# Clustered attention and two MLPs on one core: head 0's scores unsplit, GpSimd's wide passes in halves, one written-out order

## The chip, the cores and the metric

The kernel runs on one core of a Trainium2 chip. The metric is device microseconds of one execution. Before the change the median of three runs is 760.87 us (759.79 to 761.59). The profile is of one further execution, which took 763.72 us itself, with a span of 761.8 us from the first to the last instruction.

## The reference

Three parts run one after the other on float32 data.

```python
# attention: 2 batches x 8 heads = 16 heads, 768 positions, 64 wide
mask = q_assign[:, :, :, None] == k_assign[:, :, None, :]   # argmax over 16 centroids
scores = np.where(mask, scale * np.matmul(q, k.transpose(0, 1, 3, 2)), -1e9)
attn = softmax(scores)                # max, exp, sum
x = (attn @ v) reshaped to [1536, 512]
# first MLP
h = ((x @ w1) * (x @ w2)) @ w3 @ w_out        # 512 -> 1024 -> 1024 -> 512
# second MLP
h = x @ w_in ; g = h * clip(h + 3, 0, 6) / 6 ; out = g @ w_out   # 512 -> 2048 -> 512
```

## The kernel before, in words

A float32 product is built from float32r matmuls. Each operand is split into a high part and a rest, and three products (high by high, high by rest, rest by high) are summed in PSUM. The split costs an ACT copy (the high part) and a DVE or POOL subtraction (the rest) for every tile.

**Attention.** The 16 heads follow one another. For head h, `load_qk` (L1167) loads q and k, `qk_T` transposes them on PE, `qk_hi` and `qk_lo` split them, DMAs (`move_kh`, `move_kl`, `move_qh`) put the parts of k and q where a single matmul sums two of the three products, `assign_mm` (L1228) multiplies by the centroids, and nine steps `oh0` to `oh8` on DVE and POOL make a one-hot code of the cluster, which is appended to q and k (`Ck`, `Cq`), so that the mask comes out of the score matmul. `scores` (L1323) makes one chunk of 128 queries by 768 keys in two parts, `S1` (512 keys) and `S` (256). Chunks alternate between the halves of one PSUM tile of three banks, so that neighbours share the middle bank: `S` of a chunk waits for the exp of the chunk before. `smax` (L1340) takes the row maximum on DVE, `sexp` (L1348) the exp on ACT, with the row sum. `p_T` transposes the exp, `p_hi` and `p_lo` (L1379) split it, `av` (L1382) multiplies by v.

Head 0 is an exception in the kernel before (`WHOLE = 1`): its exp and v are left whole in float32, so that its `av` is a plain float32 matmul, which the profile shows as two instructions each, and it has no `p_lo`. Its scores are split as all others are.

Two heads make a pair. For a pair, POOL adds the two halves of the sums (`o_sum`, L1412, the operation `os`), multiplies by the reciprocal of the row sums (`pair_mul`, L1443, `pm`), and DVE or POOL splits the result (`pair_hi`, `pair_lo`, L1457, `xh` and `xl`). Each of these is one pass over 128x768.

**The MLPs.** Beside the attention, weights arrive from HBM, and five steps on ACT, POOL and DVE convert each tile of 128x512: `c0` (ACT), `c1` (`c_clamp`, L1567, a POOL pass), `c2` (ACT), `c3` and `c5` (DVE, two SBUF inputs each). w3 is multiplied by w_out ahead (`w`, L1629), then x by w1 and w2 (`ab`, L1705, batch 0; `b`, L1957, batch 1), then by that product (`x2`, L1820). The second MLP takes 16 steps: `h` (L2268) seven products for a block of w_in, with snapshots and sums on ACT and DVE between them, `hr`, `hm`, `hh`, `hl` the activation and its split, `o` (L2312) the product with w_out. The splits of its operands are `xs` (`x_sum`, L2229), `xwl` (`x_lo`, L2235), `Ll` (`l_lo`, L2182) and `wol2` (`w_lo`, L2192), on DVE or POOL.

**The order.** Every operation is an entry of `Plan` with an engine (or a choice of engines), a duration, what it needs, a due time and the buffers that it takes and gives back. `Plan.order` (L888) is a planner: it steps through time with these durations and latencies, and of the operations that can start takes the one due first. A table `SHIFT` with one number for nearly every operation moves the due times. Each engine then executes its operations in the order in which the planner emitted them; nothing overtakes.

`warm` (L1089) is a one-column activation that exists to bring a table into ACT: `root` does it with Sqrt, `warm` with Exp. `idle_pe` (L1117) issues matmuls without use, 21 in all.

Of the kernel before, what the change touches and what calls it, by code (L numbers as in the profile page):

```python
# [44 lines left out]
SHIFT = {  # L45
    "id": 8.27, "root": -37.83, "warm": -0.72, "cenl": -28.31, "cen1": -21.13, "cen2": -11.74, "cen3": 0.22,
    ("idle", 0): 0.14, ("idle", 1): 14.27, ("idle", 7): -19.93, ("idle", 8): 1.32, ("cT", 0): -2.63,
    ("cTc", 0): -18.72, ("cTc", 1): 38.21, ("lq", 0): -20.58, ("lk", 0): -6.84, ("vhi", 0): 13.43,
    ("vlo", 0): -8.33, ("T", 0, 0): -2.21, ("qkh", 0, 0): -20.39, ("qkl", 0, 0): -48.81, ("T", 0, 1): 58.8,
# [820 lines left out]
class Plan:  # L870
# [10 lines left out]
    def op(self, key, eng, dur, fn, need=(), due=0.0, take=(), drop=(), lat=0.0, lock=False, after=()):  # L881
        assert key not in self.ops, key
        if isinstance(eng, str):
            eng, dur = (eng,), (dur,)
# [1535 lines left out]
```

## Time and profile before

| | us |
|---|---|
| median of the runs | 760.87 |
| profiled execution | 763.72 |
| its span | 761.8 |
| PE busy | 739.7 |
| DVE busy | 617.8 |
| ACT busy | 551.5 |
| POOL busy | 209.9 |

A line of the timeline gives the start and the length in us, the engine, the line of the kernel, the operation, the tile written and the tiles read, the form, and in brackets how long the engine had been idle and what released it. POOL is GpSimd, DVE is VectorE, ACT is ScalarE, PE is TensorE. SPq is the queue that issues the DMAs. A matmul's length is its latency; matmuls that follow one another overlap.

### The profile page before, as it was taken

Reading aid. Unit: us, or ns where it says so; the run is one execution under the profiler, and the core shown is the slowest. Engines: PE = TensorE matmul, PEld = TensorE weight load, DVE = VectorE, ACT = ScalarE, POOL = GpSimd, SP = SyncE. Lnnn points to the kernel's source line nnn. Section 1 sums busy time; section 2 is a strip of 40 time slices with the busy share of each in tenths; the row PEclk is TensorE's granted clock in tenths of the full one; section 3 lists DMA queues with packets and bytes.
Section 4 is the critical chain, followed back from the end, with each engine's and each line's share of the span. In section 5 each row is a group of like instructions: output and inputs, shape, how many; then the busy total and the mean of one; then the engine's idle time right before and its main releaser. Section 6 shows DMA issues by size and latency. Waiting matters only on the chain.

```text
span 761.8 us, 12047 instructions
## 1 busy us (share of the span) xinstructions
PE 739.7 (97%) x4143; PEld 673.7 (88%) x4143; DVE 617.8 (81%) x1032; ACT 551.5 (72%) x1037; POOL 209.9 (28%) x232
## 2 busy tenths in 40 slices
PE   5899998999999999999999999999999999999998
PEld 4679887889899998999999999988988888988896
DVE  7778898999988887878896998979878867676642
ACT  6788898888889777878756767668765756565553
POOL 2441645252445435351341301322203000000000
PEclk9999999999999999999999999999999999999999
DMA  8745554565546646342536534685431224222102
GB/s 223 225 128 163 146 146 118 156 160 136 151 124 173 170 127 182 113 137 84 159 100 193 178 125 139 196 264 192 157 103 37 76 70 135 83 60 78 47 1 97
DMA packets 81740, 101.96 MB, mean 134 GB/s; under 512 B 30960, under 2 KB 56592, under 8 KB 81680
## 3 DMA queue, kind: packets, MB, share of 16 engines
q1 hardware_dynamic: 81680, 101.20, 45.0%
q8 instruction: 33, 0.54, 0.3%
q14 instruction: 27, 0.22, 0.1%
HBM read 71.34 MB, written 15.78 MB: 114 GB/s over the span
## 4 chain that ended last, share of the span: by engine, by line
PE 82%; DVE 6%; ACT 5%; DMA 4%; issue 2%; SPq 0%; POOL 0%; DVEq 0%; ACTq 0%; POOLq 0%
PE po L2312 15%; PE psh L2268 13%; PE av L1390 8%; PE psx L1820 8%; PE pst L1332 8%; PE ptr L1367 7%; PE psab L1705 7%; PE psab L1957 7%; PE psw L1629 5%; DMA qkn<-in_k_dram 1%; PE pa L1233 1%; PE ptqk L1194 1%; DVE den L1344 1%; PE pt L1601 1%; DMA rdb<-rd 1%
## 5 line engine op out<-in xcount | busy, mean ns | idle before, releaser
L1569 POOL TENSOR_SCALAR cvt<-cvt 128x512 f32<-128x512 f32 x72 | 67.3, 938 | 192.0 <-ACT cvt L1013 178.1
L1344 DVE TENSOR_REDUCE den<-pst 128x1 f32<-128x768 f32 x96 | 91.5, 953 | 22.8 <-PE pst L1332 18.1
L1351 ACT ACTIVATE p<-pst,den 128x768 f32<-128x768 f32 x96 | 86.6, 902 | 17.8 <-DVE den L1344 16.9
L1010 DVE TENSOR_TENSOR pl<-ptr,ph 128x512 fp32r<-128x512 f32 x135 | 89.4, 680 | 9.4 <-ACT ph L1013 9.1
L1013 ACT ACTIVATE ph<-ptr 128x512 fp32r<-128x512 f32 x135 | 78.7, 596 | 18.6 <-PE ptr L1367 13.8
L1367 PE MATMUL ptr<-id_f,p 128*128 128x128 f32 x576 | 81.3, 272 | 0.9 <-DVE pl L1010 0.6
L1705 PE MATMUL psab<-xT,abhl 128*128 128x384 f32 x384 | 78.9, 342 | 0.3 <-ACT asb L1013 0.3
L1367 PEld LDWEIGHTS ptr<-id_f,p 128*128 128x128 f32 x576 | 68.2, 140 | 8.8 <-DVE pl L1010 0.9
L1332 PE MATMUL pst<-kk,qkL 128*128 128x512 f32 (+1 forms) x192 | 71.0, 378 | 3.1 <-ACT p L1351 3.0
L1705 PEld LDWEIGHTS psab<-xT,abhl 128*128 128x128 f32 x384 | 66.2, 188 | 2.3 <-ACT asb L1013 0.8
L1332 PE MATMUL pst<-kk,qkH 128*128 128x512 f32 (+1 forms) x192 | 64.9, 342 | 0.0
L1390 PE MATMUL av<-pl,vs 128*128 128x384 f32 x180 | 61.3, 341 | 2.3 <-DVE pl L1010 2.3
L1390 PE MATMUL av<-ph,vs 128*128 128x384 f32 x180 | 63.3, 351 | 0.2 <-ACT T L1013 0.2
L1578 DVE SCALAR_TENSOR_TENSOR cvs<-cvt,cvs 128x512 int32<-128x512 int32 x72 | 52.4, 735 | 12.7 <-ACT cvs L1013 6.4
L1013 ACT ACTIVATE cvt<-raw 128x512 f32<-128x512 f32 x72 | 48.2, 672 | 11.5 <-DVE cvs L1582 3.8
L2290 ACT ACTIVATE tt<-m_sn,three 128x384 f32<-128x384 f32 x48 | 29.4, 615 | 37.0 <-DVE m_sn L2278 27.7
L1013 ACT ACTIVATE cvs<-raw 128x512 int32<-128x512 uint8 x72 | 47.9, 673 | 6.7 <-DMA set<-cvs 5.2
L1582 DVE SCALAR_TENSOR_TENSOR cvs<-cvt,cvs 128x512 int32<-128x512 int32 x72 | 51.2, 719 | 0.4
L1629 PE MATMUL psw<-woh,wT 128*128 128x512 f32 x128 | 49.3, 411 | 0.0
L1332 PEld LDWEIGHTS pst<-kk,qkL 128*128 128x128 f32 x192 | 36.9, 192 | 9.8 <-ACT p L1351 8.0
L1013 ACT ACTIVATE m_sn<-psh 128x384 f32<-128x384 f32 x64 | 30.8, 483 | 20.0 <-PE psh L2268 19.9
L2312 PE MATMUL po<-m_whl,m_gv 128*128 128x512 f32 x153 | 40.6, 392 | 0.6 <-DVE m_gv L1010 0.6
(198 smaller groups left out, 1829.6 us busy)
## 6 DMA issues: line engine op xcount, KB each, us to landing
raw<-in_moe_w_dram SPq DMA_DIRECT2D x32, 512.0 KB, 3.6
m_gb<-set SPq DMA_DIRECT2D x64, 256.0 KB, 3.3
raw<-in_moe_w_out_dram SPq DMA_DIRECT2D x24, 512.0 KB, 3.5
raw<-in_moe_w_in_dram SPq DMA_DIRECT2D x16, 512.0 KB, 5.1
set<-cvs SPq DMA_DIRECT2D x32, 256.0 KB, 3.1
kk<-qkH SPq DMA_DIRECT2D x16, 384.0 KB, 4.2
abp<-cvs SPq DMA_DIRECT2D x16, 256.0 KB, 2.3
b_gv<-abp SPq DMA_DIRECT2D x16, 256.0 KB, 4.4
```

The source lines that it names most:

```text
L1010: nc.vector.tensor_tensor(out=out, in0=a, in1=b, op=ALU.subtract)
L1013: nc.scalar.activation(out=out, in_=in_, func=AF.Copy, **kw)
L1332: x = mm(out=psr[:, t, ks_], lhsT=TT[nm, h][:, i, cs_], rhs=flat(TT["K", h][:, a])[:, ks_], start=st, stop=sp)
L1344: done["mx", n] = [other_banks(nc.vector.tensor_reduce(out=den_at(h, 0, c), in_=psS[h, c], axis=AX.X, op=ALU.max, negate=True), ("S", n + 1))]
L1351: done["ex", n] = [other_banks(nc.scalar.activation(out=flat(p), in_=psS.pop((h, c)), func=AF.Exp, bias=den_at(h, 0, c), accum_out=den_at( ...
L1367: nc.tensor.transpose(pt[:, blk(j)], pps[h, 3 * hf + c][:, blk(kb)], id_f)
L1390: mm(out=t[:, 0:HF], lhsT=vs_t[h][:, 2 * s + i, :], rhs=x_[:, c0:c0 + HF], start=(s == 0 and i == 0 and n == 0), stop=(s == 2 and i == 1 a ...
L1569: (nc.gpsimd.tensor_scalar if e == "pool" else ts)(out=tf, in0=tf, scalar1=H_MAX, scalar2=-H_MAX, op0=ALU.min, op1=ALU.max)
L1629: mm(out=ps, lhsT=wT[m, hf][:, a, blk(kk)], rhs=w_[hf][:, kk, :], start=(kk == 0 and n == 0), stop=(kk == 3 and n == 2))
L1705: mm(out=ps[:, 0:HF], lhsT=s[:, w, a, blk(kk)], rhs=xT0[0][:, x_, kk, hf * HF:hf * HF + HF], start=(kk == 0 and n == 0), stop=(kk == KD - ...
L2268: mm(out=ps[:, 0:HF], lhsT=left(p, l, a, kk), rhs=x[:, x_, kk, :], start=(st and kk == 0 and m == 0), stop=(kk == 1 and m == 2), skip_grou ...
L2312: mm(out=outs[b, c], lhsT=g[:, a, blk(c % 3)], rhs=w[:, w_, :], start=(first and a == 0 and w_ == 0), stop=(last and a == 1))
```

## The change

The planner, its latencies and `SHIFT` go. `RANK` gives every operation its place in one list of 3968, and `ON` the engine where there is a choice. The families are listed in the order in which their operations are created (by head, by chunk, and so on). `order` sorts by rank and asserts that needs and buffers hold.

```diff
-SHIFT = {
-    "id": 8.27, "root": -37.83, "warm": -0.72, "cenl": -28.31, "cen1": -21.13, "cen2": -11.74, "cen3": 0.22,
...
+RANK = {
+    "id": "7",
+    "root": "246",
+    "warm": "217",
...
+    "idle": "12 58 109 137 39 47",
...
+    "lq": "2 4 36 76 151 457 321 616 709 946 927 1188 1180 1430 1613 1668",
+    "lk": "11 19 62 146 361 486 519 714 773 965 970 1216 1388 1466 1650 1719",
+    "lv": "1 14 169 399 602 673 475 808 919 1224 1117 1462 1386 1580 1742 1900",
...
+    "os": "349 415 619 688 854 917 1111 1169 1397 1419 1610 1693 1954 1965",
+    "pm": "429 439 695 707 931 936 1178 1182 1439 1447 1674 1740 1975 1983 2157 2164",
...
+    "xwl": "2707 2758 2750 2746 2767 2779 2776 3100 3245 3185 3270 3225 3239 3369",
+    "xs": "2716 2726 2754 2761 3132 3218 3219 3280",
...
+ON = {
+    "Ck": "da",
+    "Cq": "aa",
+    "oh1": "ppppppppppdppdd",
+    "oh4": "ppdppppppppppdp",
+    "xh": "ppap",
+    "c1": "ppdpddppdppppdppppppppppppppdpppppppppdpdddpddddpppppppppdddpddpddddpddp",
...
+    "Ll": "ddddddddddddddddddpddpdddddddppd",
+    "wol2": "ddddpdddddddddpppppddddpddddpddp",
+    "xwl": "pddddddddddpdp",
+    "xs": "ddddpppp",
```

Of `c1`, 25 of 72 passes go from POOL to DVE. Of the passes of the second MLP's splits that POOL does, `wol2` goes from 3 to 9, `xs` from 2 to 4, `xwl` from 1 to 3, `Ll` from 3 to 4 (one `xwl` lies in the first MLP's time). In the new list `root` stands between the exp of chunks 2 and 3 of head 1 (ranks 241 and 261), and the first exp of all has rank 94, ahead of `warm`. The first DMAs are in the order centroids, v of head 0, q of head 0, a tile of w3, q of head 1, k of head 0; before, they were centroids, q of head 0, a tile of w3, k of head 0.

Head 0's scores become plain float32, without `qk_lo`, `move_kl` and `move_qh`; its `assign_mm` too. The odd chunks put their 256 keys into a bank of another pool, so that no neighbours share one, and have two maxima, a minimum over both, two exps and two sums, which `den_whole` adds. Its exp and v are split as in the other heads (`WV = 0`).

```diff
+    WHOLE, WV = 1, 0
...
+        if h < WHOLE:
+            o = W_["sm"] = ps_a.tile([128, 512], F32, tag="a", name="pss") if t and part else None
+            ks_ = slice(512, 768) if part else slice(0, 512)
+            o = o[:, 0:256] if t and part else psr[:, t, 256:768] if t else psr[:, t, ks_]
+            x = mm(out=o, lhsT=TT["H", h][0:80, i, cs_], rhs=flat(TT["K", h][0:80, 1]).bitcast(F32)[:, ks_], start=True, stop=True)
...
+            big, small = psS[h, c]
+            done["mx", n] = [other_banks(nc.vector.tensor_reduce(out=den_at(h, 0, c), in_=big, axis=AX.X, op=ALU.max, negate=True), ("S", n + 1))]
+            nc.vector.tensor_reduce(out=den_at(h, 2, c), in_=small, axis=AX.X, op=ALU.max, negate=True)
+            tt(out=den_at(h, 0, c), in0=den_at(h, 0, c), in1=den_at(h, 2, c), op=ALU.min)
```

`os`, `pm` and `xl` become two operations each, one for each half of 384 columns, and what follows waits for the half that it needs.

```diff
-    def o_sum(pr):
-        nc.gpsimd.tensor_tensor(out=Ts[pr], in0=Ts[pr], in1=W_["o"], op=ALU.add)
+    def o_sum(pr, hf):
+        nc.gpsimd.tensor_tensor(out=Ts[pr][:, hf], in0=Ts[pr][:, hf], in1=W_["o"][:, hf], op=ALU.add)
...
-                       [("abl", j, w), ("xl", kk)] + ([("ab", j, hf, w, kk - 1)] if kk else []),
+                       [("abl", j, w), ("xl", kk, hf)] + ([("ab", j, hf, w, kk - 1)] if kk else []),
```

The sums for pair 1 (ranks of `os` and `pm`) come at 619, 688, 695 and 707, with other POOL operations between the first two and between the last two.

## Rows read from the trace of the kernel before

**Rows 1.** The page, part 1: busy time, share of the span and instructions.
```profile
PE 739.7 (97%) x4143; PEld 673.7 (88%) x4143; DVE 617.8 (81%) x1032; ACT 551.5 (72%) x1037; POOL 209.9 (28%) x232
```

**Rows 2.** Busy time by stretch: start:end, length, PE, PEld, DVE, ACT, POOL, clock, DMA.
```profile
0.00:40.00 40.00, 29.38 (x132) 21.75 (x133) 30.13 (x61) 27.69 (x51) 16.01 (x43) 0.96 0.80 223
...
40.00:60.00 20.00, 19.96 (x101) 15.27 (x100) 15.76 (x26) 17.70 (x36) 8.20 (x12) 1.00 0.48 137
...
100.00:140.00 40.00, 36.93 (x221) 32.59 (x220) 36.34 (x60) 34.40 (x69) 17.43 (x21) 0.96 0.58 159
140.00:205.00 65.00, 64.97 (x406) 57.69 (x405) 61.18 (x103) 55.92 (x112) 24.45 (x29) 1.00 0.54 139
...
375.00:500.00 125.00, 124.23 (x712) 122.83 (x711) 111.83 (x187) 83.53 (x145) 29.23 (x19) 1.00 0.50 161
500.00:742.00 242.00, 238.68 (x1191) 213.46 (x1190) 181.42 (x307) 154.67 (x279) 26.24 (x19) 1.00 0.30 97
...
124.10:127.40 3.30, 3.30 (x12) 2.90 (x11) 1.73 (x3) 2.88 (x7) 3.22 (x4) 0.50 0.00 0
```

**Rows 3.** Waits of PE: total us, times, longest.
```profile
PE av L1390 <- DVE pl L1010: 2.3, 1, 2.3
```

**Rows 4.** Timeline, 117 to 125 us.
```profile
117.41 1.81 POOL L1413 TENSOR_TENSOR T<-T,O 128x768 f32<-128x768 f32 x1 [0.50 <-DMA rdb<-rd]
...
118.24 1.27 DVE L1010 TENSOR_TENSOR pl<-ptr,ph 128x512 fp32r<-128x512 f32 x2
...
119.30 1.83 POOL L1448 TENSOR_TENSOR T<-T,rdb 128x768 f32<-128x768 f32 x1
...
119.43 2.85 DVE L1582 SCALAR_TENSOR_TENSOR cvs<-cvt,cvs 128x512 int32<-128x512 int32 x2
...
123.80 0.49 PE L1390 MATMUL av<-pl,vs 128*128 128x384 f32 x1 [2.26 <-DVE pl L1010]
```

**Rows 5.** Groups of instructions by line: count, busy us, mean ns, idle before.
```profile
L1010 DVE TENSOR_TENSOR pl<-ptr,ph 128x512 fp32r<-128x512 f32 x135 | 89.4, 680 | 9.4 <-ACT ph L1013 9.1
```

**Rows 6.** The chain that ended last: start us, us, what.
```profile
2.57 4.31 DMA qkn<-in_k_dram
...
42.35 1.17 PE pst L1332 x6
...
47.02 1.29 PE av L1390 x4
...
138.35 1.40 PE av L1390 x8
```

**Rows 7.** Timeline, ACT table loads and the tile that the first activation reads.
```profile
0.73 1.28 ACT L1092 ACT_TABLE_LOAD   x1 [0.73 <-PEq L2404]
...
0.80 0.06 DVE L1073 MEMSET three<- 128x1 f32 x1 [0.80 <-PEq L2404]
...
9.17 1.28 ACT L1092 ACT_TABLE_LOAD   x1
```

**Rows 8.** Timeline of the start: first and sixth row maximum.
```profile
21.46 0.96 DVE L1344 TENSOR_REDUCE den<-pst 128x1 f32<-128x768 f32 x1 [0.70 <-PE pst L1332]
...
35.63 0.95 DVE L1344 TENSOR_REDUCE den<-pst 128x1 f32<-128x768 f32 x1
```

**Rows 9.** Timeline, 574 to 584 and 640 to 645 us.
```profile
575.87 2.01 POOL L1007 TENSOR_TENSOR m_whl<-x2f,m_whl 128x768 fp32r<-128x768 f32 x1 [22.80 <-ACT m_whl L1013]
576.10 2.20 DVE L1010 TENSOR_TENSOR m_gv<-tt,m_gv 128x384 fp32r<-128x384 f32 x1
...
578.35 0.50 PE L2312 MATMUL po<-m_whl,m_gv 128*128 128x512 f32 x1 [0.62 <-DVE m_gv L1010]
...
640.72 1.57 POOL L1007 TENSOR_TENSOR m_gB<-m_gb,m_gB 128x512 fp32r<-128x512 f32 x1 [45.16 <-PE po L2312]
641.05 1.78 DVE L1010 TENSOR_TENSOR m_hl<-m_gb,m_hl 128x512 fp32r<-128x512 f32 x1
...
643.96 1.32 PE L2268 MATMUL psh<-m_whl,m_w 128*128 128x384 f32 x6 [0.69 <-DVE m_sn L2278]
```

More of the change, by code (lines that the diff above doesn't have):

```diff
@@ L884, in op @@
             eng, dur = (eng,), (dur,)
-        self.ops[key] = [key, dict(zip(eng, dur)), None, fn, tuple(need), due + SHIFT.get(key, 0.0), tuple(take), tuple(drop), lat,
+        self.ops[key] = [key, dict(zip(eng, dur)), None, fn, tuple(need), due, tuple(take), tuple(drop), lat,
             len(self.ops), lock, tuple(after)]
     def order(self):
-        delta, bias = 0.05, {"dve": 0.3, "pool": -0.3}
-        ops = self.ops
-        left, users, src = {}, {}, {}
+        ops, pos, n, m = self.ops, {}, {}, {}
@@ L892, in order @@
+        rank = {f: v.split() for f, v in RANK.items()}
         for k, o in ops.items():
-            left[k] = len(o[4]) + len(o[11])
-            src[k] = []
-            for n in o[4]:
-                users.setdefault(n, []).append((k, True))
-            for n in o[11]:
-                users.setdefault(n, []).append((k, False))
-        slots = {r: [0.0] * c for r, c in self.rings.items()}
-        free = dict.fromkeys(ENG, 0.0)
-        port = {"dve": 0.0, "pool": 0.0}
-        ready = {k: None for k, o in ops.items() if not left[k]}
@@ L903, in order @@
-        out = []
-        while len(out) < len(ops):
-            cand = {e: [] for e in ENG}
-            for k in ready:
-                o = ops[k]
-                t = 0.0
-                ok = True
-                for r in set(o[6]):
-                    c = o[6].count(r)
-                    if len(slots[r]) < c:
-                        ok = False
-                        break
-                    t = max(t, sorted(slots[r])[c - 1])
-                if not ok:
-                    continue
-                best = None
-                for e, d in o[1].items():
-                    st = max(free[e], t)
-                    for end, pe in src[k]:
-                        st = max(st, end + LAT.get((pe, e), 0.08))
-                    if e == "pool":
-                        st = max(st, port["dve"])
-                    elif e == "dve" and o[10]:
-                        st = max(st, port["pool"])
-                    f = st + d + bias.get(e, 0.0)
-                    if best is None or f < best[0]:
-                        best = (f, e, st)
-                cand[best[1]].append((best[2], o[5], o[9], k))
-            pick = None
-            for e in ENG:
-                if cand[e]:
-                    m = min(cand[e])[0] + delta
-                    c = min((d, st, i, k) for st, d, i, k in cand[e] if st <= m)
-                    if pick is None or c[1] < pick[0]:
-                        pick = (c[1], c[3], e)
-            if pick is None:
-                raise RuntimeError(f"no operation can start after {len(out)} of {len(ops)}")
-            st, k, e = pick
-            o = ops[k]
-            o[2] = e
-            del ready[k]
-            for r in o[6]:
-                slots[r].remove(min(slots[r]))
-            end = st + o[1][e]
-            free[e] = end
-            if e == "pool" or e == "dve" and o[10]:
-                port[e] = end
-            for r in o[7]:
-                slots[r].append(end + 0.3)
-            out.append(k)
-            for u, data in users.get(k, ()):
-                if data:
-                    src[u].append((end + o[8], e))
-                left[u] -= 1
-                if not left[u]:
-                    ready[u] = None
@@ L959, in order @@
-        return [ops[k] for k in out]
+            f = k[0] if isinstance(k, tuple) else k
+            pos[k] = int(rank[f][n.setdefault(f, 0)])
+            n[f] += 1
+            o[2] = next(iter(o[1]))
+            if len(o[1]) > 1:
+                o[2] = {"a": "act", "d": "dve", "p": "pool"}[ON[f][m.setdefault(f, 0)]]
+                m[f] += 1
+            assert o[2] in o[1], k
+        seq = sorted(ops.values(), key=lambda o: pos[o[0]])
+        room = dict(self.rings)
+        for i, o in enumerate(seq):
+            assert pos[o[0]] == i, o[0]
+            assert all(pos[x] < i for x in o[4] + o[11]), o[0]
+            for r in o[6]:
+                room[r] -= 1
+                assert room[r] >= 0, (o[0], r)
+            for r in o[7]:
+                room[r] += 1
@@ L962, in cluster_attention_moe_kernel @@
+        return seq
 @with_exitstack
@@ L1231, in assign_mm @@
             c0 = 128 * (h % H) + 32 * (1 - hf)
-            for n, x in enumerate("HL"):
-                mm(out=pa[:, 0:HF], lhsT=cT[:, c0:c0 + 128], rhs=TT[x, h][:, hf], start=hf + n == 0, stop=hf + n == 2)
+            for n, x in enumerate("H" if h < WHOLE else "HL"):
+                c = cT[:, c0:c0 + 128]
+                mm(out=pa[:, 0:HF], lhsT=c.bitcast(F32) if h < WHOLE else c, rhs=TT[x, h][:, hf], start=hf + n == 0,
+                   stop=hf + n == (1 if h < WHOLE else 2))
     N2 = 2 * NC
@@ L1334, in scores @@
                 done.setdefault(("S", n), []).append(other_banks(x, ("mx", n - 1), ("ex", n - 1)))
+        if h < WHOLE:
+            o = W_["sm"] = ps_a.tile([128, 512], F32, tag="a", name="pss") if t and part else None
+            ks_ = slice(512, 768) if part else slice(0, 512)
+            o = o[:, 0:256] if t and part else psr[:, t, 256:768] if t else psr[:, t, ks_]
+            x = mm(out=o, lhsT=TT["H", h][0:80, i, cs_], rhs=flat(TT["K", h][0:80, 1]).bitcast(F32)[:, ks_], start=True, stop=True)
+            if not (t and part):
+                done.setdefault(("S", n), []).append(other_banks(x, ("mx", n - 1), ("ex", n - 1)))
+            else:
+                psS[h, c] = psr[:, t, 256:768], o
     def den_at(h, i, c):
@@ L1350, in sexp @@
         n = NC * h + c
+        pps[h, c] = flat(p)
+        if isinstance(psS[h, c], tuple):
+            big, small = psS.pop((h, c))
+            done["ex", n] = [other_banks(nc.scalar.activation(
+                out=flat(p)[:, 0:512], in_=big, func=AF.Exp, bias=den_at(h, 0, c), accum_out=den_at(h, 1, c)
+            ), ("S", n + 1))]
+            nc.scalar.activation(out=flat(p)[:, 512:768], in_=small, func=AF.Exp, bias=den_at(h, 0, c), accum_out=den_at(h, 2, c))
+            return
         done["ex", n] = [other_banks(nc.scalar.activation(
@@ L1423, in den_add, with den_whole @@
         nc.scalar.activation(out=d[:, 2, :], in_=d[:, 1, :], func=AF.Copy, bias=1e-9)
+    def den_whole(pr):
+        x = dens[pr][:, :, 1:WHOLE * NC:2]
+        tt(out=x[:, 1], in0=x[:, 1], in1=x[:, 2], op=ALU.add)
     def den_recip(pr):
@@ L1509, in attn_ops @@
             pr = h // 2
-            op(("dd", pr), "act", 0.2, lambda: den_add(pr), [("ex", h - i, c) for i in range(2) for c in range(NC)], due=e + 0.9)
+            exs = [("ex", h - i, c) for i in range(2) for c in range(NC)]
+            if pr == 0:
+                op(("dx", pr), "dve", 0.1, lambda: den_whole(pr), exs, due=e + 0.9)
+                exs = [("dx", pr)]
+            op(("dd", pr), "act", 0.2, lambda: den_add(pr), exs, due=e + 0.9)
             op(("dr", pr), "dve", 0.2, lambda: den_recip(pr), (("dd", pr),), due=e + 1)
@@ L1911, in cluster_attention_moe_kernel @@
         d = T(6 + 3.5 * k_)
-        nd = [("pm", KD + i) for i in range(KD)]
+        nd = [("pm", KD + i, x) for i in range(KD) for x in range(2)]
         if k_ >= 3:
@@ L2058, in g1_lo @@
         sub_on(e, gh1[1][:, 1, r, :], gb1[0][:, r, :], gh1[1][:, 0, r, :])
-    last1 = [("bg1", J1 - 1), ("b", J1 - 1, 6, 1)]
+    last1 = [("bg1", j) for j in range(J1)] + [("b", J1 - 1, 6, 1)]
     X1 = B0 + BP * J1 + 0.2
```

369 lines of the change are left out of this document (205 added, 164 removed), and 821 rows, old and new, of tables (RANK, SHIFT).

## The prediction, made before the run

> **What bounds the kernel now.** I read the page's busy times first: PE is busy for 739.7 of 761.8 us [rows 1], so a change pays only by taking work from PE or by closing one of its few gaps. Then the busy time by stretch [rows 2], to see where the gaps lie: 10.6 us in the first 40 (40.00 less 29.38), 3.1 between 100 and 140, none to speak of from 140 to 205, 0.8 from 375 to 500, 3.3 from 500 to 742. Between 124.1 and 127.4 PE is busy throughout, but the granted clock is 0.50, which is 1.2 GHz. So four places count: the start, 100 to 140, the second MLP, and the last write, which the change leaves as it is.
>
> The list of PE's waits names the largest single one after the start: 2.3 us, `av` for `pl` [rows 3]. The timeline tells how it came about [rows 4]. POOL does two passes of 128x768 back to back, `os` from 117.41 and `pm` from 119.30, 1.8 us each. DVE's two `pl`, which read PSUM and one SBUF tile, run beside the first at their usual speed (1.27 for two, against a mean of 0.68 for one [rows 5]). The two `c5` behind them read two SBUF tiles and take 2.85 us together, where a two-input pass over 128x512 takes the 0.68 of rows 5: about 1.5 us is waiting, until `pm` ends. The row maximum and the next two `pl` queue behind them, and PE stands from 121.5 to 123.80. After that gap its clock falls to half for the stretch of 3.3 us in rows 2.
>
> **The change, part by part.**
>
> *Halves and the new places of `os` and `pm`.* For pair 1 the passes no longer touch each other: four halves of some 0.92 us (half of 1.83 [rows 4]) stand at ranks 619, 688, 695 and 707. The DVE operations that the ranks put beside the last three are maxima, `qkl`, `wc` and `wtl`, all with a PSUM input, which the rows show unhindered; `c3` and `c5` stand well apart. I take the 2.26 us gap [rows 4] and the half clock behind it away: 3.3 us at half speed are 1.7 us lost. Together 4.0 us. Bounds: nothing, if DVE is late there all the same, and 4.8, the stretch's whole idle time of 3.1 and the 1.7. I take 4.0, since the other gaps there are small and have other causes. The late consequence: DVE is full from 140 on (61.18 of 65.00) while PE loses nothing there, so earlier arrivals need not be given back.
>
> *Head 0 on PE.* Two chained score parts of 512 and one of 256 columns, each a pair of float32r matmuls, take 1.17 us for 2560 columns [rows 6], so a chunk of 1536 took 0.70. A float32 matmul of 384 columns takes 1.29 / 2 = 0.645 (four instructions are two matmuls [rows 6]), so 768 columns take 1.29. Six chunks: +3.5 us. `assign_mm`: four float32r matmuls of 0.175 (1.40 for eight [rows 6]) become two of 0.645, +0.6. `av`: twelve of 0.645 become 24 of 0.175, 7.74 to 4.20, -3.5. The sum is +0.6 of work, but the parts lie in different places: the added scores lie in the first 40 us, where PE has 10.6 idle, the saved `av` behind them, where PE is full (19.96 of 20.00 [rows 2]). So the question is how late the chain of head 0 ends. From its first row maximum (21.46) to the end of its sixth (36.58) it takes 15.1 us [rows 8]. In the new ranks DVE's queue between the same two holds about as much: no wait for the shared bank, but three odd chunks with 0.35 us more of maxima each (an estimate from the 0.96 of a 768 wide one) and a `pl` of 0.68. What moves is its beginning. k of head 0 was issued at 2.57 and landed 4.31 later [rows 6]; now v of head 0 and q of head 1, 0.2 MB each, go ahead of it, at 223 GB/s [rows 2] 1.8 us. `assign_mm` adds 0.6 (1.2 at half clock), the first chunk up to 1.2. Against that `qkl` and two DMAs fall out of the chain. I take the chain 1.5 us late, bounds 0.7 and 2.4. The 3.5 us saved of `av` less this: -2.0, between -2.8 and -1.1.
>
> *Table loads.* The kernel before has two, 1.28 us each, both at the start [rows 7]. `root` (Sqrt) now stands between two exps of head 1, so there are four: one ahead of the first exp, one for `root`, one back. A load does not wait for what its activation reads: the one at 0.73 starts before that tile is written at 0.80 [rows 7]. So the load ahead of the first exp hides in the wait for the row maximum. The other two are 2.6 us on ACT in a stretch where it has 2.3 us free in 20 [rows 2]; the exps behind it hold the scores of head 1, and those PE. Bounds 0 (a load more cannot gain) and 2.6; I take 0.9, what is left if two thirds fall into ACT's free time. The Trainium skill, "ScalarE: Activation LUTs", section "What ACT_TABLE_LOAD costs", speaks against this part more strongly: a switch costs a drain of about 1.38 us beside the load; by it the two would be 5.3 us. Rows 7 show loads of 1.28 and no drain of their own.
>
> *`c1`, `pl` and the rest on DVE.* Nine `pl` more for head 0 (6.1 us) less its two `qkl`; 25 `c1` move from POOL. No row shows one on DVE; the nearest is the two-input 128x512 of rows 5, 0.68, for an operation of one input an upper end, and half of it is my lower one: 8 to 17 us, 19 of the 25 after 300 us of PE work. From 375 to 500 DVE has 13.2 us free; I cost this at nothing, cover being that slack, and at up to 2 us if it is gone; fewer POOL passes there could as well give a little, up to 1.
>
> *More POOL passes in the second MLP.* Long passes (1.2 us and more) behind 470 us of PE work go from 9 to 19 (`wol2`, `xs`, `xwl`, `Ll`); these are not halved. The trace has the price of three: beside passes of 2.01 and of 1.57 us DVE's subtractions take 2.20 and 1.78 where one over 128x512 has 0.68 [rows 5], and PE waits 0.62 and 0.69 [rows 9]. That is 1.31 us for nine passes, 0.15 each; ten more, 1.5. DVE sheds work for it where it is far from full (181.42 of 242 [rows 2]), which gives a little back: +1.2. Bounds 0 and 7 (0.7 each, the dearest row).
>
> The sum: -4.0 - 2.0 + 0.9 + 1.2 = -3.9. The profiled execution took 763.72, 2.85 above the median of the runs; the same step from the median gives 760.87 - 3.9 = **757.0 us**.
>
> **The rivals.**
>
> *Slower: the blocked port moves to the second MLP.* Ten more long passes, several in a row (three of `xs` and `xwl` at ranks 3218 to 3225), each holding DVE for up to 1.65 us. For it: every gap of PE over 0.6 us behind 510 us comes right after such a pass [rows 9]. Against it: PE has two to six microseconds of other work between most snapshots and their users. At 0.7 each it costs 7.0 instead of 1.2, and the time is 762.8; if the start gains nothing either, 763.9. It decides from 0.5 us a pass on, where the other terms (-5.1) are used up. Chance 0.22.
>
> *No change: DVE takes it back.* With the gap at 121.5 closed, the `c3`, `c5` and `pl` of the next 80 us still have to pass a DVE that is 94% full, and the gap comes elsewhere; only the clock's 1.7 stays. 760.87 - 1.7 - 1.1 + 1.2 = 759.3 to 760.5. Chance 0.12.
>
> *No change: a table switch costs what the page says.* With a drain, 5.3 us on ACT instead of 2.6, nothing of the difference hidden: 757.0 + 2.7 = 759.7. This is the rule of the page named above. Against it: ACT has idle time that takes some of it, and rows 7 show no more than 1.28. Chance 0.04.
>
> *Much faster: head 0 runs ahead.* Chunks in separate banks let PE work through its scores without waiting, the table loads hide, and the late passes cost nothing: -4.0 - 2.8 = -6.8, 754.1, down to 750 if the whole 4.8 near 120 and the 3.3 us of gaps in the second MLP go too. Chance 0.22.
>
> **How the numbers follow.** The forecast has 0.40 and, by itself, 755.2 to 759.3. The measurement tells about 0.2% from no change, 1.5 us: faster is below 759.3, slower above 762.4. Faster takes the forecast and the last rival, 0.62; same the two in the middle, 0.16; slower the first, 0.22. The range goes from 751, near the low end of the last rival, to 764.5, just past the dear end of the first.
>
> **What the profile will show.** Right: no PE wait of over 1 us and no half clock near 120, `c5` there under 1.7 us for two; four table loads, two near 45 us; PE's idle time from 100 to 140 under 1 us; head 0's `pst` at 1.3 us a chunk with no wait for `p` between chunks; k of head 0 landing after 8 us. Wrong: PE idle in the second MLP grown beyond 5 us, a gap near 45 us of over 2 us, or the first exp later than 25 us.

## The result: 1.4% slower, and the profile after

The changed kernel takes 772.35 us (median of 4 runs, 771.85 to 774.74), the kernel before 761.23 beside it: a ratio of 1.0139 (95% interval 1.0113 to 1.0165). Forecast were 757.0 and a range of 751 to 764.5. The profiled execution took 774.74, the slowest of the four; its span is 772.6, 10.8 more than before, and two single profiles can differ by more than the medians do.

The page's busy times and the busy time by stretch (columns as in [rows 2]) of the changed kernel:

```profile
PE 745.8 (97%) x4143; PEld 675.7 (87%) x4143; DVE 621.2 (80%) x1065; ACT 549.5 (71%) x1043; POOL 201.3 (26%) x234
```

```profile
0.00:40.00 40.00, 31.65 (x106) 20.10 (x107) 28.79 (x66) 25.47 (x47) 14.81 (x41) 0.91 0.69 198
40.00:60.00 20.00, 18.01 (x114) 15.56 (x113) 18.20 (x31) 19.20 (x39) 6.15 (x9) 1.00 0.49 133
...
100.00:140.00 40.00, 39.58 (x247) 34.85 (x245) 39.36 (x67) 36.40 (x74) 19.90 (x26) 1.00 0.58 160
...
205.00:300.00 95.00, 89.59 (x560) 83.72 (x559) 75.32 (x124) 71.43 (x145) 38.66 (x46) 0.98 0.53 142
...
500.00:742.00 242.00, 238.32 (x1188) 214.23 (x1187) 170.69 (x299) 150.25 (x275) 41.40 (x21) 0.99 0.29 97
```

PE's idle time near 120 us is gone (39.58 of 40.00, clock 1.00; it was 36.93 and 0.96). The new hole is one that the prediction did not look at, 205 to 300 us: 5.41 us idle, where the kernel before has 0.33:

```profile
205.00:300.00 95.00, 94.67 (x605) 89.93 (x604) 80.37 (x132) 77.69 (x158) 42.04 (x45) 1.00 0.58 154
```

Where the time went is read best at instructions that both kernels have. The table gives the start of the n-th row maximum (16 heads of six; one in two pieces counts once), of the second MLP's first matmul (`psh`) and of the last matmul, from the timelines. The last column is run e10 below, the changed kernel with its faults of order repaired.

| point | before | changed | difference | e10 |
|---|---|---|---|---|
| 1st row maximum | 21.46 | 23.74 | +2.3 | 22.11 |
| 6th | 35.63 | 39.22 | +3.6 | 37.24 |
| 24th | 102.23 | 105.85 | +3.6 | 101.59 |
| 36th | 146.43 | 145.41 | -1.0 | 141.55 |
| 60th | 225.28 | 226.09 | +0.8 | 222.24 |
| 61st | 228.77 | 233.09 | +4.3 | 225.78 |
| 96th | 358.58 | 365.34 | +6.8 | 354.37 |
| first `psh` | 502.38 | 511.38 | +9.0 | 500.21 |
| last matmul | 757.81 | 768.61 | +10.8 | 754.37 |

By stretch, with the forecast in brackets: to the 24th maximum +3.6 (-2.0 + 0.9 = -1.1), from there to the 60th -2.8 (-4.0), from there to the second MLP **+8.2 (0)**, the second MLP +1.8 (+1.2). Of the 14.7 us between the forecast -3.9 and the measured +10.8, 8.2 lie in the third stretch and 4.7 in the first.

The largest stall, in the timeline of the changed kernel from 214 to 232 us:

```profile
217.79 0.68 DVE L1037 SCALAR_TENSOR_TENSOR cvs<-cvt,cvs 128x512 int32<-128x512 int32 x1
...
220.55 0.57 DVE L680 STREAM_TRANSPOSE cd<-ohs 128x384 f32<-128x384 f32 x1
...
221.14 1.18 SPq L639 DMA_DIRECT2D kk<-cd  x2
...
224.11 0.82 SPq L1005 DMA_DIRECT2D raw<-in_moe_w_dram  x1
...
224.98 0.50 SPq L1149 DMA_DIRECT2D abp<-cvs  x1
...
229.18 0.66 ACT L423 ACTIVATE cvs<-raw 128x512 int32<-128x512 uint8 x1 [3.36 <-DMA abp<-cvs]
...
230.68 0.90 ACT L793 ACTIVATE p<-pst,den 128x768 f32<-128x768 f32 x1
...
231.73 0.66 PE L808 MATMUL ptr<-id_f,p 128*128 128x128 f32 x4 [3.23 <-ACT p L793]
```

The last conversion step of a weight chunk ends at 218.47, and its write to DRAM (`abp`) could go. It goes at 224.98. On SP's queue it stands behind the one-hot codes of head 10 (`kk<-cd`), which wait until DVE has transposed them (220.55 to 221.12), two more DMAs, and a load of raw weights that waits until ACT has read its buffer. A buffer of `cvs` (there are two) is free only when the write has landed, here at 229.10, so ACT's next conversion waits 3.36 us, and with it all that is queued behind it on ACT: two high parts, an exp. PE stands 3.23 us for that exp, and from 232.35 to 235.77 its clock is at 0.50, 1.2 GHz. In the list of ranks the write has 1307, its last conversion step 1264. Over the 16 such writes of the first MLP the distance is 33.8 ranks on average (one of 295 raises it; the median is 11.5), with 3.8 other DMAs between; in the order that the planner of the kernel before makes it is 7.6 ranks (median 6.5) and 0.7 DMAs.

The second MLP, 557 to 570 us:

```profile
557.22 9.63 POOL L417 TENSOR_TENSOR x2f<-x2f 128x768 f32<-128x768 f32 x2 [9.85 <-DVE m_gA L420]
...
563.26 1.89 DVE L1037 SCALAR_TENSOR_TENSOR cvs<-cvt,cvs 128x512 int32<-128x512 int32 x1
...
565.08 2.19 DVE L1749 SCALAR_TENSOR_TENSOR tt<-tt,m_sn 128x384 f32<-128x384 f32 x1
...
569.73 2.82 PE L1723 MATMUL psh<-m_x,m_gB 128*128 128x384 f32 x9 [2.36 <-DVE tt L1749]
```

Two running sums (`xs`) on POOL end at 566.85. DVE's `tt`, 0.55 us elsewhere (569.93), takes 2.19, to 567.27, and PE waits 2.36. The start, with the three later table loads:

```profile
8.64 0.66 PE L605 MATMUL ptqk<-id_f,qkn 128*128 128x128 f32 x2 [2.31 <-DMA qkn<-in_k_dram]
...
20.78 4.63 PE L758 MATMUL pst<-kk,qkH 80*128 80x512 f32 x6 [1.25 <-ACT qkH L423]
...
23.21 1.28 ACT L793 ACT_TABLE_LOAD   x1
23.74 0.96 DVE L778 TENSOR_REDUCE den<-pst 128x1 f32<-128x768 f32 x1 [1.37 <-PE pst L758]
...
39.22 0.69 DVE L774 TENSOR_REDUCE den<-pst 128x1 f32<-128x512 f32 x1 [0.70 <-ACT p L793]
...
53.12 1.28 ACT L503 ACT_TABLE_LOAD   x1
54.41 0.20 ACT L503 ACTIVATE warm<-three 128x1 f32<-128x1 f32 x1
...
56.65 1.28 ACT L793 ACT_TABLE_LOAD   x1
...
58.98 0.38 PE L751 MATMUL pst<-kk,qkL 128*128 128x256 f32 x1 [0.91 <-ACT p L793]
```

### The profile page after: what moved, and what is told of

It reads as the page before. It is cut to its first block, busy times and chain, and to the rows that moved or that the text cites. A ratio compares the mean times of both kernels' runs of the same rounds, so it can differ in the third digit from the quotient of the medians.

```text
span 772.6 us, 12046 instructions
## 1 busy us (share of the span) xinstructions
PE 745.8 (97%) x4143; PEld 675.7 (87%) x4143; DVE 621.2 (80%) x1065; ACT 549.5 (71%) x1043; POOL 201.3 (26%) x234
## 4 chain that ended last, share of the span: by engine, by line
PE 71%; DVE 14%; ACT 6%; DMA 4%; issue 3%; SPq 1%; POOL 1%; ACTq 0%; DVEq 0%; POOLq 0%
PE po L1767 13%; PE psh L1723 12%; PE psx L1275 9%; PE psab L1412 6%; PE pst L751 6%; PE av L831 6%; PE ptr L808 6%; PE psw L1084 5%; PE psab L1160 4%; DVE pl L420 2%; DVE den L778 2%; DMA abp<-cvs 1%; ACT p L793 1%; PE pa L649 1%; DVE cvs L1033 1%
## 5 line engine op out<-in xcount | busy, mean ns | idle before, releaser
L778 DVE TENSOR_REDUCE den<-pst 128x1 f32<-128x768 f32 x93 | 88.5, 952 | 20.4 <-PE pst L751 17.7
L420 DVE TENSOR_TENSOR pl<-ptr,ph 128x512 fp32r<-128x512 f32 x144 | 96.1, 681 | 10.4 <-ACT ph L423 9.6
L423 ACT ACTIVATE ph<-ptr 128x512 fp32r<-128x512 f32 x144 | 83.5, 596 | 19.2 <-PE ptr L808 15.1
L1160 PE MATMUL psab<-xT,abhl 128*128 128x384 f32 x384 | 84.0, 348 | 0.7 <-DVE g L1170 0.7
L1024 POOL TENSOR_SCALAR cvt<-cvt 128x512 f32<-128x512 f32 x47 | 32.4, 693 | 150.8 <-ACT cvt L423 120.5
L831 PE MATMUL av<-ph,vs 128*128 128x384 f32 x192 | 68.6, 357 | 0.0
L751 PE MATMUL pst<-kk,qkL 128*128 128x512 f32 (+1 forms) x180 | 67.0, 374 | 1.6 <-ACT p L793 1.4
L831 PE MATMUL av<-pl,vs 128*128 128x384 f32 x192 | 65.2, 340 | 0.0
L751 PE MATMUL pst<-kk,qkH 128*128 128x512 f32 (+1 forms) x180 | 60.1, 339 | 0.6 <-DMA qkH<-cd 0.6
L1745 ACT ACTIVATE tt<-m_sn,three 128x384 f32<-128x384 f32 x48 | 29.3, 615 | 25.7 <-DVE m_sn L1733 10.8
L1767 PE MATMUL po<-m_hl,m_gv 128*128 128x512 f32 x153 | 42.7, 398 | 0.5 <-DVE m_gv L420 0.5
```

The costliest lines, as they stand in the source:

```text
L420: nc.vector.tensor_tensor(out=out, in0=a, in1=b, op=ALU.subtract)
L423: nc.scalar.activation(out=out, in_=in_, func=AF.Copy, **kw)
L751: x = mm(out=psr[:, t, ks_], lhsT=TT[nm, h][:, i, cs_], rhs=flat(TT["K", h][:, a])[:, ks_], start=st, stop=sp)
L778: done["mx", n] = [other_banks(nc.vector.tensor_reduce(out=den_at(h, 0, c), in_=psS[h, c], axis=AX.X, op=ALU.max, negate=True), ("S", n + 1))]
L831: mm(out=t[:, 0:HF], lhsT=vs_t[h][:, 2 * s + i, :], rhs=x_[:, c0:c0 + HF], start=(s == 0 and i == 0 and n == 0), stop=(s == 2 and i == 1 a ...
L1160: mm(out=ps[:, 0:HF], lhsT=s[:, w, a, blk(kk)], rhs=xT0[0][:, x_, kk, hf * HF:hf * HF + HF], start=(kk == 0 and n == 0), stop=(kk == KD - ...
```

## The experiments

Sixteen runs, each a single edit or a set of them. Most move an operation in the list of ranks, by a list of (operation, what it stands behind):

```diff
+        names = [o[0] for o in seq]
+        for k, behind in MOVE:
+            names.remove(k)
+            names.insert(names.index(behind) + 1, k)
+        pos = {k: i for i, k in enumerate(names)}
+        seq = [ops[k] for k in names]
```

The list sits above, so line numbers in their rows are higher by its length. My theory after the result: late writes make the stretch from 205 to 500. The rival: VectorE, which has 25 clamps and nine low parts more.

**One late write (e1).**

```diff
+MOVE = [
+    (('abp', 1, 1), ('c5', 'ab', 1, 1)),
+]
```

> One rank changed: the write of the converted chunk ab 1 1 stands right behind its last conversion step instead of 43 ranks later. Theory (late writes: the write waits on SP's queue behind moves that are not ready, ACT stands 3.36 us at its next conversion until the write has landed, PE stands 3.23 us at 228.5 and works 3.4 us at half clock behind it): the gap and the half clock go, 3.2 + 1.7 = 4.9 us less, some 767.4. Rival (DVE, which has 9 more low parts and 25 more clamps, is the bound there, and the write is late because DVE is): the same 772.3, with a gap of PE of the same size within some microseconds.

770.94 us (ratio 1.0113, 1.0088 to 1.0139), 1.4 less, which is within the noise of two such medians. The profile tells more. PE's waits from 205 to 300 us:

```profile
PE ptr L819 <- DVE qkL L627: 1.6, 1, 1.6
PE pst L762 <- DMA qkH<-cd: 1.0, 1, 1.0
```

The gap and the half clock at 228 are gone, as the theory says, but from the 60th maximum to the first `psh` only 2.9 us of the 4.9 arrive (282.39 against 285.29). The next late write takes most of the rest: ACT waits 2.21 us for it and PE 1.64 behind that, little more than in the changed kernel (2.06 and 1.48), but now the clock falls there (half from 272.36 to 275.77, 1.7 us lost):

```profile
268.38 0.66 ACT L434 ACTIVATE cvs<-raw 128x512 int32<-128x512 uint8 x1 [2.21 <-DMA abp<-cvs]
...
270.69 0.66 PE L819 MATMUL ptr<-id_f,p 128*128 128x128 f32 x4 [1.64 <-DVE qkL L627]
```

**All late writes (e2).** The 13 with two or more other DMAs between them and their last conversion step: nine of `abp` and four of `sst`, the same write for weights of the second MLP.

```diff
+MOVE = [
+    (('abp', 0, 0), ('c5', 'ab', 0, 0)),
+    (('abp', 1, 1), ('c5', 'ab', 1, 1)),
...
+    (('sst', 15, 1), ('c5', 'set', 15, 1)),
+]
```

> All 13 writes with two or more other DMAs between them and their last conversion step stand right behind that step. Theory of late writes: besides the 4.9 us of the one at 225 us the waits of ACT of 2.06 us at 272 and of 0.60 at 320 go, with PE's 1.48 at 275.3, and a part of what PE loses between 245 and 285 in smaller gaps: 7 to 8 us less, 764 to 765. Rival (DVE is the bound): 772, or no more than 1 us less. If only the first write matters: 767.4, as with that one alone.

767.24 us (1.0069, 1.0045 to 1.0093), 5.1 less. From the 60th maximum (226.79) to the first `psh` (505.87) it now loses 2.0 us against the kernel before, where the changed kernel loses 8.2. ACT has no wait for a write left between 205 and 300 us.

**The clamps back on GpSimd (e9).** The rival.

```diff
-    "c1": "ppdpddppdppppdppppppppppppppdpppppppppdpdddpddddpppppppppdddpddpddddpddp",
+    "c1": "pppppppppppppppppppppppppppppppppppppppppppppppppppppppppppppppppppppppp",
```

> All 72 clamps on GpSimd, as in the kernel before; all else as in the changed kernel. Theory (the stretch from 205 to 500 us is lost to late writes, not to the 25 clamps on VectorE): no gain, 772 to 775, with the gaps at 228 and 275 as they are. Rival (VectorE is the bound there): 3 to 8 us less, 764 to 769, and the gap at 228 gone or under 1 us.

774.08 us (1.0148, 1.0123 to 1.0174). The two longest gaps from 205 to 300 us stay, and the rival falls, as far as it is the clamps:

```profile
PE ptr L808 <- ACT p L793: 2.8, 1, 2.8
PE ptr L808 <- DVE qkL L616: 1.7, 1, 1.7
```

**Table loads (e4).**

```diff
+MOVE = [
+    ('root', 'cen1'),
+    ('warm', ('qkh', 0, 1)),
+]
```

> The square root that warms its table stands in front, ahead of the centroids' square root, and the exp that warms its table behind the second high part of head 0, as in the kernel before: two table loads instead of four. Theory (the two loads near 53 and 58 us are on ACT's way to the scores and cost what PE falls behind between 54 and 62 us, 2.2 us): 2.2 us less, 770.1. Rival (PE falls behind there because head 0 ended late and DVE is full): no change, 772.3. By the price with a drain, 5.3 us, the gain could be up to that.

772.45 us (1.0147, 1.0123 to 1.0170): nothing. Yet in its trace the 24th maximum comes at 103.22 instead of 105.85, and of PE's waits between 45 and 200 us only one of 0.3 is left. Part of the 2.6 us is lost again later: the gap at 226 is 3.60 instead of 3.23, and at the first `psh` 1.4 us are left (509.97 against 511.38). Why the medians show none of it is open; two such medians don't tell differences under about 2.6 us.

**Running sums on VectorE (e5).**

```diff
-    "xs": "ddddpppp",
+    "xs": "dddddddd",
```

> The four running sums of the second product (128x768) that GpSimd does in the second MLP go to VectorE. Theory (blocked shared port: the pass at 564.68 holds two VectorE passes for 1.2 and 1.6 us, PE stands 2.36 us at 567.4 and works 3.4 us at half clock behind it): 2.4 + 1.7 = 4.1 us less, less up to 0.5 for four passes of 0.96 us on VectorE, some 768.5. Rival (the wait is one of the chain through ACT, and the pass only lies beside it): no change or slower by up to 1 us.

771.42 us (1.0128, 1.0108 to 1.0147), 0.9 less, within the noise. The 2.36 at 567 shrinks to 0.61; a wait of 1.41 appears at 583.6, again for a `tt`. In the profiles the second MLP, from the first `psh` to the last matmul, is 3.0 us shorter (254.27 against 257.23).

**k of head 0 first (e6).**

```diff
+MOVE = [
+    (('lk', 0), ('lq', 0)),
+    (('lv', 0), ('lk', 0)),
+]
```

> The load of k of head 0 stands right behind that of q of head 0, ahead of v of head 0, of the first weights and of q of head 1. Theory (the chain of head 0 starts late because k lands at 8.50, and PE waits 2.31 us for it): k lands some 2 us earlier, the first row maximum is 1.5 us earlier, and the time 1 to 2 us less than with the ranks as they are, some 771. Rival (the chain is held by the table of the first exp, by DVE and by float32 scores at half clock): no change, 772.4.

774.92 us (1.0169, 1.0148 to 1.0190), 2.6 more, about the noise of the two medians: neither. PE's first transposition starts at 5.59 instead of 8.64, and the first row maximum at 22.56 instead of 23.74, so the load was late as forecast; but by the sixth maximum the gain is gone (39.39 against 39.22), and 2.3 us are lost between the 60th and the 96th (141.53 against 139.25), with a half clock from 278.30 to 281.71 that the changed kernel doesn't have. Why is open.

**All repairs (e7).** The edits of e2, e4, e5 and e6, and two small ones of order (four DMAs behind the codes of head 11, a conversion near 464 us later):

```diff
+    (('dB', 9), ('Cq', 11, 1)),
+    (('ld', 'ab', 3, 0), ('Cq', 11, 1)),
+    (('ld', 'ab', 2, 1), ('Cq', 11, 1)),
+    (('lq', 13), ('Cq', 11, 1)),
...
+    (('c2', 'set', 10, 0), ('bs', 6, 2)),
+    (('ld', 'set', 12, 0), ('c2', 'set', 10, 0)),
```

> The repairs together: the 13 late writes behind their conversion steps, the two table loads taken out, the four running sums on VectorE, k of head 0 loaded first, four DMAs that stand ahead of the last codes of head 11 put behind them, one conversion near 464 us put 20 ranks later with the load behind it. If the parts are as the trace has them and add up (6 for the writes, 2.2 for the table loads, 3.5 for the sums, 1 to 1.5 each for the other three): 757 to 759, below the kernel before. If each stall that is removed is partly taken up by the next one, as the one at 228 was by that at 272: 761 to 765. If the clock at the start decides: 764 to 768.

761.59 us (0.9989, 0.9976 to 1.0003).

**The same without the edit of e6 (e10).**

> The repairs together but without the early load of k of head 0, which by itself cost 2 us (774.9 against 772.4): 759.5 to 760.5, some 0.2% below the kernel before. If that load costs nothing beside the other repairs: 761.6, the same.

**760.25 us (0.9976, 0.9964 to 0.9987): faster than both kernels**, 0.2% below the one before and 12.1 us below the changed one. No wait of PE over 0.9 us is left between 40 and 570 us:

```profile
205.00:300.00 95.00, 94.10 (x601) 88.97 (x600) 81.60 (x137) 76.03 (x154) 37.52 (x46) 1.00 0.58 155
```

**One repair left out at a time (e14 to e17).** The set of e10 without the edit of e4, of e2, of e5, and without the six lines above.

> The repairs without the early load, less one: the two table loads near 53 and 58 us are back. Their price in a kernel whose later stalls are gone. Forecast of the prediction 0.9, the trace of the changed kernel 2.2 in its stretch, the run that took them out alone 0.1. If a stall's price shows once nothing behind it takes it up: 2.2 more than the repairs, 762.5. If ACT has room for them: 760.3 to 761.

> The repairs less the 13 late writes, which stand at their late ranks again. By the run that moved them alone 5 to 6 us more, 765.5 to 766; by the trace of the changed kernel (the gap of 3.23 and half a clock of 3.4 us at 228, the gap of 1.48 at 275) up to 7, 767.

> The repairs less one: the four running sums of the second product are GpSimd's again. The trace of the changed kernel gives 2.36 us of gap and 1.7 of clock, less 1.4 that a new gap at 575 takes back: 2 to 3 us more than the repairs, 762.3 to 763.3. If the wait behind them is hidden elsewhere: 760.3 to 761.

> The repairs less the two small changes of order: the codes of head 11 stand behind four other DMAs again, and the conversion near 464 us stands where it was. By the gaps of 0.97 and 1.38 us in the traces: 1.5 to 2.5 us more than the repairs, 761.8 to 762.8. If they only lie where PE has other work: 760.3 to 761.

Without e2's edit PE's gaps for the exp are back (e15, 205 to 300 us):

```profile
PE ptr L826 <- ACT p L811: 2.9, 1, 2.9
PE pst L769 <- ACT p L811: 2.4, 1, 2.4
```

The price is the ratio less 0.9976, times 762:

| left out | us | ratio (95%) | price: left out of e10 | gain: repaired alone |
|---|---|---|---|---|
| table loads, e14 | 763.46 | 1.0019 (1.0003 to 1.0035) | 3.3 | -0.1 |
| late writes, e15 | 768.99 | 1.0095 (1.0079 to 1.0112) | 9.1 | 5.1 |
| sums, e16 | 764.44 | 1.0031 (1.0016 to 1.0045) | 4.2 | 0.9 |
| small order, e17 | 762.79 | 1.0008 (0.9993 to 1.0022) | 2.4 | not run |

Each price is good to about 1.5 us (the half widths of two ratios, 0.0012 and 0.0016, in squares), each figure of the last column to about 2.6. The first two prices are borne out by the profiles. The writes cost 9.7 us from the 60th maximum to the first `psh` (287.71 in e15, 277.97 in e10). Without the edit of e4 the last matmul comes 3.3 us later than in e13 below, another kernel with e4's edit, whose clock is half for the same 6.8 us near 25 us (757.79 and 754.53). The other two hold some of the start, which neither edit touches. The sums cost 2.8 in the second MLP (256.92 in e16, 254.16 in e10), and the other 1.8 us of e16's profile lie before it, where its clock is half from 19.13 to 29.37 us and e10's is full. The small order costs 0.7 at the last matmul, with the start's clock full in both profiles (755.11 and 754.37). Of the runs with a mean clock of 0.997 or more, five of e17's 12 and nine of e10's, the medians are 760.85 and 760.09. So that it costs more than that isn't shown. For the writes a single repair gives too little, since the next stall takes part of it up, as e1 shows; that the four prices together, 19.0, are more than the 12.1 may come from stalls that share a cost, but also from the start's clock.

**The product of pair 1 later, in the kernel before (e8).**

```diff
     seq_ = plan.order()
+    names = [o[0] for o in seq_]
+    names.remove(("pm", 1))
+    names.insert(names.index(("wol", 7)) + 1, ("pm", 1))
+    seq_ = [plan.ops[k] for k in names]
```

> The kernel before, with one change of order: GpSimd's product of pair 1 (128x768, whole) stands behind the low part of the eighth block of output weights, which waits for ACT, and so no longer right behind the sum of pair 1. Theory of the term at 120 us (the two passes back to back hold the two last conversion steps, PE stands 2.26 us and works 3.4 us at half clock): the gap and the half clock go, 3 to 4 us less, 757.5 to 758.5. Rival (DVE is full there, and the same work is late in another place): 761.5, with a gap of over 1 us between 115 and 145.

762.72 us (1.0009, 0.9995 to 1.0022): no gain. In the timeline:

```profile
119.71 1.28 DVE L1582 SCALAR_TENSOR_TENSOR cvs<-cvt,cvs 128x512 int32<-128x512 int32 x2
...
122.56 0.45 PE L1390 MATMUL av<-pl,vs 128*128 128x384 f32 x1 [0.75 <-DVE pl L1010]
123.45 1.83 POOL L1448 TENSOR_TENSOR T<-T,rdb 128x768 f32<-128x768 f32 x1
...
125.31 0.84 ACT L1013 ACTIVATE xT<-T 128x768 fp32r<-128x768 f32 x1 [1.75 <-POOL T L1448]
...
127.42 0.63 PE L1367 MATMUL ptr<-id_f,p 128*128 128x128 f32 x4 [1.91 <-DVE qkL L1204]
```

The two `c5` are free (1.28 against 2.85 in [rows 4]) and that gap falls from 2.26 to 0.75. But ACT's `xT` waits 1.75 us for the product that now comes later, the `qkH` queued behind it comes late, and PE stands 1.91.

**Whole passes at the new places (e13).** The set of e10, with pair 1's sum and product not halved:

```diff
     def o_sum(pr, hf):
+        if pr == 1 and hf == 0:
+            return
+        hf = slice(0, 2) if pr == 1 else slice(hf, hf + 1)
```

(`pair_mul` likewise.)

> As the repairs without the early load, with pair 1's sum and product on GpSimd as whole passes of 128x768, each at the place of its second half (ranks 688 and 707). Theory (the gap and the half clock at 120 us went because the passes are halved): the two hold VectorE again, PE loses 2 to 4 us between 115 and 145, and the time is that much more than without this. Rival (they went because the two conversion steps now stand ahead of the passes): the same, within 1 us, with no gap of PE over 0.6 us there.

760.52 us (0.9982, 0.9968 to 0.9996), as e10: the rival, with no wait of PE listed from 100 to 140 us.

```profile
122.17 2.38 POOL L888 TENSOR_TENSOR T<-T,O 128x768 f32<-128x768 f32 x1
122.18 0.68 DVE L1073 SCALAR_TENSOR_TENSOR cvs<-cvt,cvs 128x512 int32<-128x512 int32 x1
...
125.22 1.85 POOL L930 TENSOR_TENSOR T<-T,rdb 128x768 f32<-128x768 f32 x1
125.40 0.68 DVE L451 TENSOR_TENSOR wT<-pt,wT 128x512 fp32r<-128x512 f32 x1
```

The passes lie beside one `cvs` that takes its usual 0.68 and DVE operations with a PSUM input. For pair 1 it is the places, not the halves; the other pairs' halves were not taken back.

**Head 0's scores split again (e12).** The set of e10, with `WHOLE` at 0, the low parts and two moves (`qkl`, `Ek`, `Dq`) put back, each second score part behind the exp of the chunk before, and the splits of head 2's q and k behind them; all else keeps its place in an order made for unsplit scores:

```diff
+    (('qkl', 0, 0), ('qkh', 0, 1)),
...
+    (('S', 0, 1), ('ex', 0, 0)),
...
+    (('S', 0, 5), ('ex', 0, 4)),
+    (('qkh', 2, 0), ('S', 0, 5)),
...
-    WHOLE, WV = 1, 0
+    WHOLE, WV = 0, 0
```

> As the repairs without the early load, with head 0's scores split again (float32r pairs in one bank pair, each chunk's second part behind the exp of the chunk before), its low parts and the two moves for them put back behind the high parts; the output of head 0 stays in pairs. If the unsplit scores cost about what the split ones did (the forecast had the chain 1.5 us later with them): within 1.5 us of the repairs with unsplit scores. If their float32 matmuls at half clock are what head 0 loses: 2 to 3 us less. If the split ones wait for two more moves of some 3 us and for each other: 2 to 4 us more.

763.20 us (1.0022, 1.0005 to 1.0038), 3.5 us more by the ratios: the third case. PE's waits from 15 to 45 us:

```profile
PE pst L801 <- ACT p L843: 6.1, 3, 3.4
PE pst L801 <- DVE kk L515: 1.4, 1, 1.4
PE pa L699 <- DVE qkL L666: 1.3, 1, 1.3
```

**More idle matmuls (e11).** The set of e10 with eight instead of four and four instead of two.

```diff
-    op(("idle", 0), "pe", 0.0, lambda: idle_pe(4), ("id",), due=-30, take=("a",), drop=("a",))
...
+    op(("idle", 0), "pe", 0.0, lambda: idle_pe(8), ("id",), due=-30, take=("a",), drop=("a",))
...
```

> As the repairs without the early load, with six more idle matmuls in the first 20 us (eight instead of four at the start, four instead of two ahead of the second assignment), which fill waits of PE. Theory (of what head 0 costs more than forecast, 3.4 us is the half clock from 20.7 to 27.6, which lies on the float32 scores, and comes after PE's waits of 2.31, 0.47 and 1.25): the clock stays full there and the time is 1.5 to 3 us below that kernel without them. Rival (the chain of head 0 hangs on DVE and ACT, not on PE's clock): the same as without them, within 1 us.

761.51 us (0.9989, 0.9976 to 1.0002): no gain, 1.0 more by the ratios, within the noise. Its profile shows the clock full from 20 to 28 us, but so does that of e10 without them, so it does not tell what lets the clock fall there.

## Why the prediction was wrong, point by point

**The step that failed** is the part on `c1`, `pl` and the rest on DVE: "I cost this at nothing, cover being that slack". Of the engine it was right: with the clamps back on GpSimd (e9) nothing is won. But that part was nearly all that the prediction had for 205 to 500 us, and the change rewrites the order of every queue there. The prediction followed SP's queue at the start alone and took the other DMAs' ranks as harmless. A write whose rank is 43 behind its producer looks free, since nobody reads it soon; what reads its *buffer* is ACT's next conversion, and ACT carries the exps. That stretch lost 8.2 us; with the writes alone moved (e2) it loses 2.0, the time is 5.1 us less, and in an otherwise repaired kernel they cost 9.1. The sentence that DVE, full from 140 on, need not give earlier arrivals back had the same blind spot: it asked for engines only.

*Halves and new places of `os` and `pm`*: the sum was right, the credit was not. From the 24th to the 36th maximum the kernel gains 4.6 us (forecast 4.0), PE's idle time from 100 to 140 is 0.42 (forecast under 1), no half clock; 1.8 come back by the 60th. For pair 1, to which the prediction gave the 4.0, halving does nothing (e13), and moving one pass alone in the kernel before only moves the wait to ACT (e8). Which part of the new order there it takes isn't shown. The rival in which the gap comes back elsewhere is what e8 shows, though behind ACT and POOL and not a full DVE.

*Head 0 on PE*: forecast -2.0, and k 1.8 us late. k landed at 8.50, against 2.57 + 4.31 = 6.88 before, 1.6 late: right. The chain was to be 1.5 late, bounds 0.7 and 2.4; it starts 2.3 late and its sixth maximum starts 3.6 late. What was missed is the clock: it is half from 20.73 to 27.55, on the float32 scores (six matmuls take 4.63 us), twice the 3.41 us that the kernel before has at half speed there. In e10, whose profile has the clock full there, the chain starts 0.65 and its sixth maximum 1.6 late, as forecast. So the delay holds and was off by the clock, but the credit behind it was too large as well: in e10, with full clock and the table loads gone, the 24th maximum is 0.6 early and not 2.0. The other 1.4 stay open. Of the 4.7 us lost to the forecast ahead of the 24th maximum the clock has 1.0 to 1.6 (e1 and e5, with the table loads and a full clock, have that maximum at 104.88 and 104.28), the table loads 1.7. Split scores in their place cost 3.5 us more (e12), in an order not made for them, so here the unsplit ones earn their 3.5 us of matmuls.

*Table loads*: four, as forecast, with the one ahead of the first exp hidden (23.21 to 24.49, before the maximum ends at 24.70). The other two cost 2.6 us at the 24th maximum (e4) and 3.3 in the clean kernel (e14, good to 1.5), not 0.9: in a stretch where ACT has 19.20 of 20.00 busy next to nothing of them hides, and the upper bound of 2.6 was the value to take. The Trainium skill, "ScalarE: Activation LUTs", section "What ACT_TABLE_LOAD costs", adds a drain of 1.38 us to each switch; the trace doesn't agree: the load at 53.12 starts 0.02 us behind the instruction before it and ends at 54.40, and the activation behind it starts at 54.41.

*More POOL passes in the second MLP*: +1.2 forecast, +1.8 measured, but made of other pieces: one place with 2.36 of gap and a half clock from 570.27 to 573.69 (1.7 lost), while the gaps of before [rows 9] are gone. In the clean kernel the four sums cost 2.8 there (e16's profile), 0.7 a pass: a multiple of the forecast's 0.15, and its dear end. So the first rival named a true mechanism and, by luck, the right direction, but the largest part of the result comes from the writes, of which it has nothing. They don't make it alone: with them moved (e2) the kernel is still 0.7% slower than before. DVE's `tt` with two SBUF inputs ending 0.42 us after POOL's pass agrees with the Trainium skill, "SBUF — State Buffer", section "SBUF: two separate sides": DVE and GpSimd take a shared port in turn, for a whole instruction.

None of the signs that would have made it wrong came: no gap of over 2 us near 45 us (0.91 at 58.07), 3.7 us idle in the second MLP and not over 5, the first exp at 24.73 and not later than 25. They were all put where a cost had been written down. Of the signs of being right, two failed in part: the scores of head 0 ran at half clock first, and the two loads came at 53 and 57 us instead of near 45.

## What to carry to other kernels

When a change fixes the order of all operations, walk each in-order queue, SP's first, and ask of every write not who reads its data but who needs its buffer, and what the writes' queue holds ahead of it that isn't ready yet. To price several stalls, repair all of them and put back one at a time: repaired singly, the largest showed 5 of 12 us and a real 3 showed nothing, though single repairs were measured to 2.6 us only. And compare landmarks of the two profiles around the place of the edit: a difference that lies ahead of it isn't its price.

## What the runs showed that was not expected

POOL can be the one that waits. The two running sums of 557.22 take 9.63 us together, where the one at 578.90 takes 1.85; DVE runs two-input passes over SBUF through the first part of it at their usual lengths. From 563.26 on it is DVE that waits.

The clock of TensorE in the same kernel differs between executions. In the profiles of e1, e5, e10 and e17 it is full from 20 to 28 us, in those of the changed kernel, e2, e4, e9 and e13 it is half for 6.8 us. The waits of PE ahead of it are much alike: at 6 us 2.1 to 2.5 in the first group and 2.3 to 3.2 in the second, at 19 us 1.2 to 1.4 in both. Here are two profiles over the same stretch, the changed kernel's, then e10's:

```profile
20.70:27.50 6.80, 6.72 (x12) 3.91 (x13) 4.96 (x11) 5.75 (x10) 3.03 (x4) 0.50 0.99 292
```

```profile
20.70:27.50 6.80, 6.40 (x25) 3.81 (x25) 6.31 (x15) 5.54 (x12) 3.05 (x4) 1.00 0.97 298
```

Of the 12 runs of e10 the three with a mean clock of 0.994 or 0.995 took 761.55 to 762.59 us, the nine from 0.997 on 759.08 to 760.98. Neither an earlier load of k (e6) nor more idle matmuls (e11) settled what decides it.
